# A decode attention on one core: 17 rounds of TensorE's loop, placed loops, and one load of keys that waits for the load ahead

## The chip, the cores and the metric

The kernel runs on one core of a Trainium2 chip. A core has five engines with instruction streams of their own: TensorE (PE; its weight loads, PEld, overlap its matmuls), VectorE (DVE), ScalarE (ACT), GpSimd (POOL) and SyncE (SP). Loads and stores go through 16 DMA engines that work side by side. Engines and transfers are tied together by semaphores alone. The metric is the device time of one execution in microseconds (us); lower is better.

## The reference

```python
B, Hq, Hkv, Sq, Sk, D = 1, 32, 8, 1, 65536, 128
k = jnp.repeat(k, rep, axis=1)          # rep = 4 query heads for each of 8 key heads
v = jnp.repeat(v, rep, axis=1)
scores = jnp.einsum("bhqd,bhkd->bhqk", q, k) * D ** -0.5
p = softmax(scores, axis=-1)
out = jnp.einsum("bhqk,bhkd->bhqd", p, v)
```

One query position for each of 32 heads attends to 65,536 keys and values of its key head. All is bf16. Keys and values are 134 MB each, and each is read once.

## The kernel before

The work is cut into NU = 32 units: 8 key heads, HU = 4 units for each. A unit is 16,384 keys: 128 partitions with T = 128 tiles each. Its keys are one load of 4 MB into one of two buffers (`kbuf`), its values another one of 4 MB into one of two (`vbuf`). Each partition's 32 KB are contiguous in memory.

SP issues the loads in the order k0, k1, v0, k2, v1, k3, v2 and so on (`sync_engine`, lines 378 to 411). A load into a buffer that was used waits for `kfree` or `vfree`: ScalarE raises `kfree` when the last of a unit's transposed keys is about to be copied, VectorE raises `vfree` when it takes a unit's result. A load's semaphore (`krdy`, `khalf`, `vrdy`) is complete at 16, one from each DMA engine. The first and the last load of keys come in two halves, the last load of values in six pieces (`V_PIECES`, in tiles) with semaphores `vpiece`.

TensorE runs a loop of 16 rounds (lines 200 to 207). A round has the keys of an even unit, the values of the odd unit before it (not in the first round), the keys of the odd unit, the values of the even one. `pe_keys` takes 16 groups of 8 tiles: it transposes a group's tiles against an identity into one of four PSUM banks (line 132), and three groups later multiplies the transposed keys with the head's four queries (line 141). `pe_values` multiplies 128 tiles of values with the weights into one small accumulator (line 158). Behind the loop, `pe_last` does the values of unit 31, piece by piece: it transposes the outputs of the other heads first (line 173), does a small sum between the first and second piece (line 178), and handles the last 8 tiles in another layout (line 191), so that the result of the last head needs no transpose.

VectorE and ScalarE copy the transposed keys out of PSUM (lines 219 and 216, ScalarE every fourth group). VectorE also takes the maximum of a unit's scores (line 248) and does the running softmax's bookkeeping; GpSimd reduces the maximum over partitions (line 369); ScalarE computes the exponentials (line 339). `passes` writes out the first passes of VectorE and ScalarE, then a loop whose body holds four passes (one head's units), then the rest. VectorE's loop runs the passes 1 to 28, seven iterations; pass u copies the keys of unit u + 1. GpSimd's and SP's streams have no loop: all 32 units are written out.

[...] The programs are fetched in blocks by DMA transfers that the profile lists as kind "instruction".

Of the kernel before, what the change touches and what calls it, by code (L numbers as in the profile page):

```python
# [10 lines left out]
P = 128  # L11
T = 128
# [5 lines left out]
HU = 4  # L18
HALF = T // 2

V_PIECES = (64, 32, 16, 8, 4, 4)
ROWS_FROM = 120


LOOP_SLOT = 176


def on_act(j):
# [3 lines left out]
def take(e, sem, n=1):  # L32

    e.wait_ge(sem, n)
    e.sem_inc(sem, -n)  # L35


def bass_standalone__gqa_softmax__decode_kernel(nc, q, k, v, out):
    _, Hq, _, D = q.shape
    _, H, Sk, _ = k.shape  # L40
    R = Hq // H
    HR = H * R
    NU = H * HU
    assert D == P and Sk == P * T * HU and T * R == 512 and H >= 3 and NU % 2 == 0
    scale = float(D) ** -0.5
    kf, vf, qf, of = k[0], v[0], q[0, :, 0, :], out[0, :, 0, :]
# [4 lines left out]
    def sb(name, shape, dt):  # L51
        return S(nc.sbuf_tensor(name, shape, dt))

    def sem(name):
        return S(nc.semaphore(name))

    kbuf = [sb(f"kbuf{i}", [P, T * D], DT.bfloat16) for i in range(2)]
    vbuf = [sb(f"vbuf{i}", [P, T * D], DT.bfloat16) for i in range(2)]
# [10 lines left out]
    ones = sb("ones", [P, 1], DT.float32)  # L69
# [8 lines left out]
    lp = sb("lp", [P, R], DT.float32)  # L78
# [12 lines left out]
    fin = pvb[NU % 2]  # L91
# [3 lines left out]
    vrdy = [sem(f"vrdy{i}") for i in range(2)]  # L95
    vpiece = [sem(f"vpiece{i}") for i in range(len(V_PIECES))]
# [3 lines left out]
    qkd, qrdy, pvd = sem("qkd"), sem("qrdy"), sem("pvd")  # L100
    cm, cma, ng, exd, sx, lrd, lra = (sem(n) for n in ("cm", "cma", "ng", "exd", "sx", "lrd", "lra"))
    xd, xa, xg = sem("xd"), sem("xa"), sem("xg")
    q_sem, o_sem, s_x, t_z, t_id, t_if, t_qT = (
        sem(n) for n in ("q_sem", "o_sem", "s_x", "t_z", "t_id", "t_if", "t_qT"))
    t_o, s_o, t_row, t_lp, s_l, t_acc, s_fin, t_last = (
        sem(n) for n in ("t_o", "s_o", "t_row", "t_lp", "s_l", "t_acc", "s_fin", "t_last"))


    def has_k(u):
        return u + 1 < NU  # L110

    def passes(e, one, start, period, last):

        for u in range(-1, start):
            one(u)
        n = (NU - 2 - start) // period
        with e.Fori(0, n):
            for u in range(start, start + period):
                one(u)
        for u in range(start + n * period, last + 1):  # L120
            one(u)
# [24 lines left out]
    def pe_keys(pe, b):  # L146
        pend = []
        for j in range(G):
            pe_transposes(pe, b, j)
            pend.append(j)  # L150
            if len(pend) > LAG:
                pe_scores(pe, b, pend.pop(0))
        while pend:
            pe_scores(pe, b, pend.pop(0))

    def value(pe, b, t, first, last):
        vv = vbuf[b][:, :].rearrange("p (t d) -> p t d", d=D)
        return pe.matmul(pvb[b][:, 0:R], lhsT=vv[:, t, :], rhs=pts[b][:, t * R:(t + 1) * R],  # L158
                         start=t == first, stop=t == last)

    def pe_values(pe, b):
        take(pe, vrdy[b], 16)
        take(pe, exd)
        for t in range(T):
            ins = value(pe, b, t, 0, T - 1)
        ins.then_inc(pvd, 1)

    def pe_last(pe):
        b = (NU - 1) % 2
        vv = vbuf[b][:, :].rearrange("p (t d) -> p t d", d=D)  # L170
        starts = [sum(V_PIECES[:i]) for i in range(len(V_PIECES))]
        pe.wait_ge(t_o, 1)
        pe.transpose(qkb[0][0:HR - R, 0:P], oT[:, R:HR], identf[:, :]).then_inc(s_o, 1)
        take(pe, exd)
        for t in range(ROWS_FROM):
            if t == starts[1]:
                pe.wait_ge(t_lp, 1)
                pe.matmul(fin[0:R, P:P + 1], lhsT=lp[:, :], rhs=ones[:, :],
                          start=True, stop=True).then_inc(s_l, 1)
            if t in starts:  # L180
                pe.wait_ge(vpiece[starts.index(t)], 16)
            ins = value(pe, b, t, 0, ROWS_FROM - 1)
        ins.then_inc(pvd, 1)
        pe.wait_ge(t_last, 1)
        for t in range(ROWS_FROM, T):
            if t in starts:
                pe.wait_ge(vpiece[starts.index(t)], 16)
            if t == starts[-1]:
                pe.wait_ge(t_acc, 1)
                pe.matmul(fin[0:R, 0:P], lhsT=acc[:, :], rhs=identf[:, :], start=False, stop=False)  # L190
            ins = pe.matmul(fin[0:R, 0:P], lhsT=pts[b][:, t * R:(t + 1) * R], rhs=vv[:, t, :],  # L191
                            start=t == ROWS_FROM, stop=t == T - 1)
        ins.then_inc(s_fin, 1)

    def tensor_engine(pe):
        pe.wait_ge(q_sem, 16)
        pe.wait_ge(t_id, 1)
        pe.transpose(trb[0][:, 0:HR], qsb[:, :], ident[0:HR, 0:HR]).then_inc(s_x, 1)  # L198
        pe.wait_ge(t_qT, 1)
        pe.addr_align(256, offset=LOOP_SLOT, max_nops=16)  # L200
        with pe.Fori(0, NU // 2) as i:
            pe_keys(pe, 0)
            with pe.If(i > 0):
                pe_values(pe, 1)
            pe_keys(pe, 1)
            pe_values(pe, 0)
        pe_last(pe)


# [11 lines left out]
    def own(e, ins, s):  # L221
        ins.then_inc(s, 1)
        take(e, s)
# [80 lines left out]
    def vector_engine(e):  # L304
        identities(e)
        e.memset(oT[:, :], 0.0).then_inc(xd, 1)
        take(e, xd)
        e.wait_ge(s_x, 1)
        own(e, e.tensor_copy(qT[:, :], trb[0][:, 0:HR]), xd)
        next_queries(e, t_qT)  # L310
        e.sem_inc(qrdy, 1)
        passes(e, lambda u: dve_pass(e, u), 1, HU, NU - 4)
        e.sem_inc(t_o, 1)
        for u in range(NU - 3, NU):
            dve_pass(e, u)
        e.sem_inc(t_lp, 1)
        e.wait_ge(s_o, 1)
        e.tensor_copy(orow[:, :], qkb[0][0:HR - R, 0:P]).then_inc(t_row, 1)
        e.wait_ge(s_l, 1)
        e.reciprocal(rl[:, :], fin[0:R, P:P + 1]).then_inc(t_last, 1)  # L320
        take(e, pvd)
        b = (NU - 1) % 2
        e.tensor_tensor(acc[:, :], acc[:, :], pvb[b][:, 0:R], ALU.add).then_inc(t_acc, 1)
        e.wait_ge(t_last, 1)
        e.wait_ge(s_fin, 1)  # L325
        e.tensor_scalar(olast[:, :], fin[0:R, 0:P], rl[:, 0:1], None, ALU.mult).then_inc(t_last, 1)  # L326
# [30 lines left out]
    def gpsimd_engine(e):  # L357
        e.memset(ident[:, :], 0.0)
        e.memset(identf[:, :], 0.0)
        e.memset(ones[:, :], 1.0)  # L360
        e.memset(dscr[:, :], 0.0)
        e.memset(la[:, :], 0.0).then_inc(t_z, 1)
        e.wait_ge(t_z, 1)
        e.partition_all_reduce(cmaxa[:, :], la[:, :], P, bass.bass_isa.ReduceOp.max).then_inc(xg, 1)
        for u in range(NU):
            if u == 0:
                e.wait_ge(xg, 1)
            take(e, cm)
            e.partition_all_reduce(cmaxa[:, :], cmax[:, :], P, bass.bass_isa.ReduceOp.max).then_inc(cma, 1)  # L369
            if u % HU == HU - 1 and has_k(u):  # L370
                take(e, lrd)
                e.partition_all_reduce(la[:, :], lp[:, :], P, bass.bass_isa.ReduceOp.add).then_inc(lra, 1)  # L372

    def src(x, n):
        h, c = n // HU, n % HU
        return x[h, c * P * T:(c + 1) * P * T, :].rearrange("(p t) d -> p (t d)", p=P)

    def sync_engine(e):
        def pieces(buf, s, sizes, sems):
            a = 0  # L380
            for w, sm in zip(sizes, sems):
                e.dma_start(buf[:, a * D:(a + w) * D], s[:, a * D:(a + w) * D]).then_inc(sm, 16)  # L382
                a += w

        def load_k(n):
            b = n % 2
            if n >= 2:
                e.wait_ge(kfree[b], n // 2)
            if n in (0, NU - 1):
                pieces(kbuf[b], src(kf, n), (HALF, T - HALF), (krdy[b], khalf[b]))  # L390
            else:
                e.dma_start(kbuf[b][:, :], src(kf, n)).then_inc(krdy[b], 16)
                e.sem_inc(khalf[b], 16)

        def load_v(n):
            b = n % 2
            if n >= 2:
                e.wait_ge(vfree[b], n // 2)
            if n == NU - 1:
                pieces(vbuf[b], src(vf, n), V_PIECES, vpiece)  # L400
            else:
                e.dma_start(vbuf[b][:, :], src(vf, n)).then_inc(vrdy[b], 16)

        load_k(0)
        for n in range(NU - 1):
            load_k(n + 1)
            load_v(n)
        load_v(NU - 1)
        e.wait_ge(t_last, 2)
        e.dma_start(of[HR - R:HR, :], olast[:, :]).then_inc(o_sem, 16)  # L410
        e.wait_ge(o_sem, 32)
# [35 lines left out]
```

## Time and profile before

| | |
|---|---|
| time, median of 3 runs | 633.15 us (633.11 to 633.5) |
| profiled execution's own time | 632.97 us |
| its span, first to last instruction | 631.2 us |
| TensorE matmuls / weight loads busy | 520.4 / 512.3 us |
| VectorE / ScalarE / GpSimd busy | 312.4 / 182.4 / 15.9 us |
| read from memory | 268.44 MB |
| mean granted TensorE clock | 0.772 |

In the profile, a row of the order of time has the start, the duration, the engine, the line and operation, the tiles written and read, the shape and count, and in brackets the idle time of the engine ahead of it with what ended it ("PEq" is TensorE's own instruction stream, which includes its waits on semaphores; "issue" is a wait for nothing that the profile shows). A row of a window has the window, its length, the busy time of each engine with a count, the granted clock, the share of the 16 DMA engines' time, and the rate in GB/s. A row of the transfer queues has packets, MB and the share of 16 engines' time: q1 is the loads' queue, the kind "instruction" is the programs'.

### The profile page before, as it was taken

The page shows a single profiled execution, that of the slowest core. Times are in us where ns is not written, and L with a number is a line of the kernel's source. Part 1 is how long each engine was busy: PE and PEld are TensorE (multiplying, and loading weights), DVE is VectorE, ACT ScalarE, POOL GpSimd, SP SyncE. Part 2 cuts the span into 40 slices and gives each one's busy share as a digit, 9 for nine tenths or more (in the row PEclk, how much of TensorE's full clock was granted, in tenths as well). Part 3 has the DMA queues.
Part 4 walks back from the last instruction along what each step waited for, and adds up shares of the span by engine and source line. Part 5 has one row for each costly group of instructions (what it writes and reads, how often), then busy time and mean ns, then how long its engine had stood idle before and what let it go on. Part 6 is the DMA issues. An engine that isn't in the chain of part 4 may idle for free. (4 is left out here: it accounts for less than half of the span.)

```text
span 631.2 us, 27735 instructions
## 1 busy us (share of the span) xinstructions
PE 520.4 (82%) x12294; PEld 512.3 (81%) x12294; DVE 312.4 (49%) x689; ACT 182.4 (29%) x410; POOL 15.9 (3%) x49
## 2 busy tenths in 40 slices
PE   4579998879887798878798787988779887879897
PEld 4479997879887788877798787988779877779896
DVE  4445554446544456434565344654445544455552
ACT  2133322123322233221332213332223322133231
POOL 0000000000000000000000000000000000000000
PEclk9788776778776788767887677877678876788776
DMA  8999999999999999999999999999999999999996
GB/s 366 429 432 431 430 430 432 432 432 432 432 432 432 432 432 432 432 432 432 432 432 432 432 432 432 432 432 432 432 432 430 432 432 432 432 432 432 424 437 255
DMA packets 10335, 268.62 MB, mean 426 GB/s; under 512 B 1234, under 2 KB 1490, under 8 KB 1746
## 3 DMA queue, kind: packets, MB, share of 16 engines
q1 hardware_dynamic: 10232, 268.44, 99.1%
q8 instruction: 7, 0.11, 0.1%
q14 instruction: 6, 0.05, 0.0%
q10 hardware_dynamic: 90, 0.02, 0.0%
HBM read 268.44 MB, written 0.01 MB: 425 GB/s over the span
## 5 line engine op out<-in xcount | busy, mean ns | idle before, releaser
L132 PE MATMUL trb<-ident,kbuf 128*128 128x128 bf16 x4096 | 357.1, 246 | 76.1 <-PEq L35 73.3
L132 PEld LDWEIGHTS trb<-ident,kbuf 128*128 128x128 bf16 x4096 | 289.8, 112 | 78.0 <-issue 77.8
L219 DVE COPY ktb<-trb 128x1024 bf16<-128x1024 bf16 x384 | 255.2, 691 | 164.2 <-DVEq L35 163.5
L216 ACT ACTIVATE ktb<-trb 128x1024 bf16<-128x1024 bf16 x128 | 131.0, 1023 | 436.0 <-ACTq L35 436.0
L141 PE MATMUL qkb<-qcur,ktb 128*128 128x4 bf16 x4096 | 173.3, 165 | 22.5 <-PEq L35 20.5
L141 PEld LDWEIGHTS qkb<-qcur,ktb 128*128 128x128 bf16 x4096 | 156.3, 98 | 26.2 <-issue 26.0
L158 PE MATMUL pvb<-pts,vbuf 128*128 128x4 bf16 x4088 | 112.1, 165 | 4.9 <-issue 1.7
L158 PEld LDWEIGHTS pvb<-pts,vbuf 128*128 128x128 bf16 x4088 | 110.0, 101 | 6.8 <-issue 4.3
L339 ACT ACTIVATE pts<-qkb,negm 128x128 bf16<-128x128 f32 x128 | 50.8, 551 | 0.0
L248 DVE TENSOR_REDUCE cmax<-qkb 128x4 f32<-128x512 f32 x32 | 22.1, 692 | 35.2 <-DVEq L35 34.2
L339 ACT ACTIVATION_READ_ACCUMULATOR pts<-qkb,negm 128x1 f32 x128 | 36.1, 282 | 0.0
L237 DVE TENSOR_TENSOR acc<-acc,pvb 128x4 f32<-128x4 f32 x23 | 3.7, 159 | 59.8 <-DVEq L35 59.8
L369 POOL PARTITION_ALL_REDUCE cmaxa<-cmax x32 | 11.9, 370 | 506.3 <-POOLq L35 506.3
L235 DVE COPY acc<-pvb 128x4 f32<-128x4 f32 x8 | 1.3, 162 | 23.8 <-DVEq L35 23.8
L226 DVE COPY qcur<-qT 128x4 bf16<-128x4 bf16 x8 | 1.4, 170 | 10.0 <-DVEq L35 9.9
L278 DVE TENSOR_TENSOR lp<-lp,rsum 128x4 f32<-128x4 f32 x24 | 3.9, 163 | 3.5
L277 DVE TENSOR_TENSOR lp<-lp,alpha 128x4 f32<-128x4 f32 x24 | 3.9, 163 | 3.5
L264 DVE TENSOR_TENSOR dm<-m 128x4 f32<-128x4 f32 x24 | 3.9, 163 | 3.5
L335 ACT ACTIVATE alpha<-dm 128x4 f32<-128x4 f32 x24 | 4.7, 197 | 2.7 <-ACTq L35 2.7
L372 POOL PARTITION_ALL_REDUCE la<-lp x7 | 3.0, 429 | 97.0 <-POOLq L35 97.0
L198 PE MATMUL trb<-ident,qsb 32*128 32x32 bf16 x1 | 0.2, 204 | 5.1 <-DMA qsb<-in_q_dram 5.1
L198 PEld LDWEIGHTS trb<-ident,qsb 32*128 32x128 bf16 x1 | 0.1, 100 | 5.1 <-DMA qsb<-in_q_dram 5.1
(43 smaller groups left out, 32.7 us busy)
## 6 DMA issues: line engine op xcount, KB each, us to landing
vbuf<-in_v_dram SPq DMA_DIRECT2D x31, 4096.0 KB, 31.4
kbuf<-in_k_dram SPq DMA_DIRECT2D x30, 4096.0 KB, 26.8
kbuf<-in_k_dram SPq DMA_DIRECT2D x4, 2048.0 KB, 17.1
vbuf<-in_v_dram SPq DMA_DIRECT2D x1, 2048.0 KB, 17.7
vbuf<-in_v_dram SPq DMA_DIRECT2D x1, 1024.0 KB, 19.8
vbuf<-in_v_dram SPq DMA_DIRECT2D x1, 512.0 KB, 20.3
vbuf<-in_v_dram SPq DMA_DIRECT2D x1, 256.0 KB, 20.5
vbuf<-in_v_dram SPq DMA_DIRECT2D x2, 128.0 KB, 20.2
```

Of the source, the lines that this page charges most:

```text
L132: ins = pe.transpose(trb[j % NTB][:, i * P:(i + 1) * P], kv[:, t, :], ident[:, :])
L141: ins = pe.matmul(qkb[b][:, t * R:(t + 1) * R], lhsT=ktb[:, off:off + P], rhs=qcur[:, :], start=True, stop=True)
L158: return pe.matmul(pvb[b][:, 0:R], lhsT=vv[:, t, :], rhs=pts[b][:, t * R:(t + 1) * R], start=t == first, stop=t == last)
L216: e.activation(dst, trb[j % NTB][:, :], AF.Copy).then_inc(eva, 1)
L219: e.tensor_copy(dst, trb[j % NTB][:, :]).then_inc(evd, 1)
L248: e.tensor_reduce(cmax[:, :], qkb[u % 2][:, :].rearrange("p (t g) -> p g t", g=R), AX.X, ALU.max).then_inc(cm, 1)
L264: e.tensor_tensor(dm[:, :], mo[:, :], mn[:, :], ALU.subtract)
L277: own(e, e.tensor_tensor(lp[:, :], lp[:, :], alpha[:, :], ALU.mult), xd)
L278: own(e, e.tensor_tensor(lp[:, :], lp[:, :], rsum[:, :], ALU.add), xd)
L335: e.activation(alpha[:, :], dm[:, :], AF.Exp, scale=scale)
L339: ins = e.activation(pv[:, g, :], sv[:, g, :], AF.Exp, bias=negm[:, g:g + 1], scale=scale, accum_out=rsum[:, g:g + 1])
L369: e.partition_all_reduce(cmaxa[:, :], cmax[:, :], P, bass.bass_isa.ReduceOp.max).then_inc(cma, 1)
```

## The change

TensorE's loop starts at the beginning of a block of 256 and runs 17 rounds. Its round is now four conditional parts: keys of the even unit (not in round 17), values of the odd unit before it (not in the first round; in round 17 the first 64 tiles alone), then keys of the odd unit and values of the even one (neither in round 17). So the first 64 tiles of the last unit's values are multiplied by the loop's code, and `pe_last` starts with the transpose of the outputs and the small sum, and goes on at tile 64. The first piece of the last values signals `vrdy` like a whole load.

VectorE's loop is placed at 208 of 256; GpSimd's passes, and SP's loads from the second round of its order on, start at the beginning of a block of 128.

SP splits value load 4 into pieces of 102 and 26 tiles with semaphores of their own. Key load 6 is issued only when the first piece has landed on all 16 DMA engines. SP then waits for the second piece as well, raises `vrdy` for the whole load itself, and issues value load 5.

```diff
+BLOCK_PE = 256
+BLOCK = 128
+MEET = 4
+MEET_TILES = 26
+DVE_SLOT = 208
...
+    meet = [sem(f"meet{i}") for i in range(2)]
...
-    def passes(e, one, start, period, last):
+    def passes(e, one, start, period, last, align=None):
...
         n = (NU - 2 - start) // period
+        if align:
+            align()
         with e.Fori(0, n):
...
-    def pe_values(pe, b):
-        take(pe, vrdy[b], 16)
-        take(pe, exd)
-        for t in range(T):
+    def pe_values(pe, b, t0, t1):
+        if t0 == 0:
+            take(pe, vrdy[b], 16)
+            take(pe, exd)
+        for t in range(t0, t1):
             ins = value(pe, b, t, 0, T - 1)
-        ins.then_inc(pvd, 1)
+        if t1 == T:
+            ins.then_inc(pvd, 1)
...
         pe.transpose(qkb[0][0:HR - R, 0:P], oT[:, R:HR], identf[:, :]).then_inc(s_o, 1)
-        take(pe, exd)
-        for t in range(ROWS_FROM):
-            if t == starts[1]:
-                pe.wait_ge(t_lp, 1)
-                pe.matmul(fin[0:R, P:P + 1], lhsT=lp[:, :], rhs=ones[:, :],
-                          start=True, stop=True).then_inc(s_l, 1)
+        pe.wait_ge(t_lp, 1)
+        pe.matmul(fin[0:R, P:P + 1], lhsT=lp[:, :], rhs=ones[:, :],
+                  start=True, stop=True).then_inc(s_l, 1)
+        for t in range(HALF, ROWS_FROM):
...
-        pe.addr_align(256, offset=LOOP_SLOT, max_nops=16)
-        with pe.Fori(0, NU // 2) as i:
-            pe_keys(pe, 0)
+        pe.addr_align(BLOCK_PE, max_nops=0)
+        n = NU // 2
+        with pe.Fori(0, n + 1) as i:
+            with pe.If(i < n):
+                pe_keys(pe, 0)
             with pe.If(i > 0):
-                pe_values(pe, 1)
-            pe_keys(pe, 1)
-            pe_values(pe, 0)
+                pe_values(pe, 1, 0, HALF)
+                with pe.If(i < n):
+                    pe_values(pe, 1, HALF, T)
+            with pe.If(i < n):
+                pe_keys(pe, 1)
+                pe_values(pe, 0, 0, T)
         pe_last(pe)
...
-        passes(e, lambda u: dve_pass(e, u), 1, HU, NU - 4)
+        passes(e, lambda u: dve_pass(e, u), 1, HU, NU - 4,
+               lambda: e.addr_align(2 * BLOCK, offset=DVE_SLOT, max_nops=0))
...
+        e.addr_align(BLOCK, max_nops=0)          # GpSimd, ahead of its passes
         for u in range(NU):
...
+            if n == MEET + 2:                    # in load_k
+                e.wait_ge(meet[0], 16)
...
-                pieces(vbuf[b], src(vf, n), V_PIECES, vpiece)
+                pieces(vbuf[b], src(vf, n), V_PIECES, [vrdy[b]] + vpiece[1:])
+            elif n == MEET:
+                pieces(vbuf[b], src(vf, n), (T - MEET_TILES, MEET_TILES), meet)
...
             load_k(n + 1)
+            if n == MEET + 1:
+                e.wait_ge(meet[1], 16)
+                e.sem_inc(vrdy[MEET % 2], 16)
             load_v(n)
+            if n == 0:
+                e.addr_align(BLOCK, max_nops=0)
```

More of the change, by code (lines that the diff above doesn't have):

```diff
@@ L22 @@
 ROWS_FROM = 120
-LOOP_SLOT = 176
+BLOCK_PE = 256
[3 more added lines that the diff above has]
+DVE_SLOT = 208
 def on_act(j):
```

## The prediction

> **What bounds the kernel now.** I read the page first (span, transfer rate, the chain that ended last), then the order of time on TensorE where it starts on a load of keys, then the transfer rate in short windows at the end, then the transfer queues in windows.
>
> ```profile
> span 631.2 us, 27735 instructions
> ...
> PE 520.4 (82%) x12294; PEld 512.3 (81%) x12294; DVE 312.4 (49%) x689; ACT 182.4 (29%) x410; POOL 15.9 (3%) x49
> ...
> GB/s 366 429 432 431 430 430 432 432 432 432 432 432 432 432 432 432 432 432 432 432 432 432 432 432 432 432 432 432 432 432 430 432 432 432 432 432 432 424 437 255
> ...
> q1 hardware_dynamic: 10232, 268.44, 99.1%
> ...
> q8 instruction: 7, 0.11, 0.1%
> q14 instruction: 6, 0.05, 0.0%
> ...
> DMA vbuf<-in_v_dram 3%; SPq L382 0%; PE pvb L191 0%; PE pvb L190 0%; PE pvb L158 0%; DVE olast L326 0%; DVEq L232 0%; DVEq L325 0%
> ```
>
> No compute engine is full, the rate stands at 432 GB/s in nearly every slice, the queue of loads (q1) fills 99.1% of the 16 DMA engines, and the chain ends in the load of the last values. 268.44 MB at 432 GB/s is 621.4 us of the 631.2. The kernel is a stream of loads. A load counts as landed when all 16 engines have added to its semaphore, so the engine that is last sets the end. The other two queues, 13 packets called "instruction", bring the engines' programs, over the same 16 engines.
>
> TensorE's rows, from four stretches of the order of time, show how late the last engine gets:
>
> ```profile
> 8.26 1.01 PE L132 MATMUL trb<-ident,kbuf 128*128 128x128 bf16 x8 [2.94 <-PEq L35]
> ...
> 102.14 3.57 PE L132 MATMUL trb<-ident,kbuf 128*128 128x128 bf16 x32 [2.22 <-PEq L35]
> ...
> 587.86 1.44 PE L132 MATMUL trb<-ident,kbuf 128*128 128x128 bf16 x12 [2.88 <-PEq L35]
> ...
> 627.24 0.29 PEld L158 LDWEIGHTS pvb<-pts,vbuf 128*128 128x128 bf16 x8 [0.16 <-DMA vbuf<-in_v_dram]
> ```
>
> These are starts that waited for a landing: the first half of key load 0, key load 5, key load 30, and the fourth piece of the last values. From load 5 to load 30 lie 50 loads: (587.86 - 102.14) / 50 = 9.714 us each. By that pace, load 5 (9.5 loads after the first half) should come at 8.26 + 92.3 = 100.5; it comes 1.6 us later. The fourth piece ends 8 tiles of 128 short of four loads after load 30: 587.86 + 38.86 - 0.61 = 626.1; it comes 1.1 us later. So the last engine lost about 2.7 us, 1.6 early and 1.1 at the end.
>
> The rate in short windows at the end (last number of each line; the one before it is the share of the engines' time) shows that it was indeed one engine:
>
> ```profile
> 624.00:624.50 0.50, 0.50 (x25) 0.50 (x23) 0.00 (x0) 0.00 (x0) 0.00 (x0) 0.50 0.99 367
> ...
> 625.50:626.00 0.50, 0.50 (x24) 0.50 (x23) 0.00 (x0) 0.00 (x0) 0.00 (x0) 0.50 0.48 166
> ...
> 626.50:627.00 0.50, 0.42 (x16) 0.42 (x16) 0.00 (x0) 0.00 (x0) 0.00 (x0) 0.50 0.06 23
> ...
> 627.00:627.50 0.50, 0.42 (x15) 0.34 (x11) 0.00 (x0) 0.00 (x0) 0.00 (x0) 0.50 0.06 19
> ```
>
> One engine's share of 432 is 27 GB/s. The first engines are done soon after 624, under half are left at 625.75, and for the last us before 627.5 a single one works (share 0.06, one in 16).
>
> What delayed it? The queues in the windows 13 to 60, 110 to 600 and 604 to 607 us (packets, MB, share of 16 engines' time):
>
> ```profile
> q8 instruction: 6, 0.10, 0.8%
> ...
> q14 instruction: 2, 0.02, 0.0%
> ...
> q14 instruction: 1, 0.01, 0.7%
> ```
>
> Nine of the program's packets lie there: six of 16 KB early (0.8% of 47 x 16 us, 1.0 us each on its engine), two in the long middle, and one of 8 KB at 605 (0.7% of 48 us, 0.34 us). That last one is the only one in the stretch in which the last engine lost 1.1 us, so I price an 8 KB fetch, with what it upsets, at 1.1. The other two in the middle fell on engines that were ahead: the 50 loads keep their pace.
>
> **The change, part by part.** *Loops placed, early branches, 17 rounds.* This takes away TensorE's and VectorE's waits for code, such as these:
>
> ```profile
> 25.79 3.04 PE L132 MATMUL trb<-ident,kbuf 128*128 128x128 bf16 x27 [3.20 <-PEq L35]
> ...
> 31.64 0.44 PE L132 MATMUL trb<-ident,kbuf 128*128 128x128 bf16 x5 [2.81 <-issue]
> ...
> 46.32 3.09 PE L158 MATMUL pvb<-pts,vbuf 128*128 128x4 bf16 x111 [1.69 <-issue]
> ...
> PE trb L132 <- PEq L35: 73.3, 28, 3.3
> ```
>
> They are worth nothing on the path: TensorE goes on to wait for keys 28 times, 2.6 us each (last row), and the stream does not stop for it. The three added branches a round lie in the same waits. If that cover were gone, a round would lose at most one such 2.8.
>
> *The end of the program.* The first 64 tiles of the last values become round 17; the transpose of the outputs and the small sum, earlier before and between the pieces, come behind them.
>
> ```profile
> 621.65 0.37 PE L173 MATMUL qkb<-identf,oT 128*28 128x128 f32 x1
> ...
> 622.84 1.87 PE L158 MATMUL pvb<-pts,vbuf 128*128 128x4 bf16 x64 [0.82 <-DMA vbuf<-in_v_dram]
> ...
> 624.64 0.19 PE L178 MATMUL pvb<-ones,lp 128*4 128x1 f32 x2
> ...
> 625.35 1.01 PE L158 MATMUL pvb<-pts,vbuf 128*128 128x4 bf16 x32 [0.52 <-DMA vbuf<-in_v_dram]
> ```
>
> The piece ends near 624.6; 0.37 and 0.19 us follow, in a gap of 0.5. A branch or two can make the next piece 0.2 to 0.5 late, and the 0.16 to 0.3 us that TensorE waits before each of the two pieces behind it take that back: 0. A late entry here would cost 2.8 less about 1.1 of such gaps, +1.7, and I take 0 because the code left behind the loop is shorter by 64 tiles. The transposed outputs go out about 1 us later, hidden by the final store.
>
> *Fetches moved.* VectorE's loop body, counted from the code, is some 180 instructions for four passes. The diff aligns by 128 instructions, on TensorE by 256, and the packets are of 8 and 16 KB: I take a packet as one such block. Put at slot 208 of 256, it ends just inside the block (from slot 384) that then also holds the tail, so the 605 fetch goes to the end of the loop's first iteration, whose last copies are these:
>
> ```profile
> 112.55 1.99 DVE L219 COPY ktb<-trb 128x1024 bf16<-128x1024 bf16 x3 [0.53 <-DVEq L35]
> ...
> 605.18 0.16 DVE L237 TENSOR_TENSOR acc<-acc,pvb 128x4 f32<-128x4 f32 x1 [2.51 <-DVEq L35]
> ```
>
> GpSimd's and SP's fetches go to the first microseconds. A moved fetch still takes its 0.34 us, and its 1.1, from the engine that carries it; if that engine is the last one, it is as late as before. Price: 0, with -1.1 as the other end (it falls on another engine, or while its engine idles) and +1.1 (on an engine that is last already).
>
> *The hold.* Key load 6 waits for 102 of the 128 tiles of value load 4; value load 5 then waits for the rest.
>
> ```profile
> 94.78 0.33 SPq L392 DMA_DIRECT2D kbuf<-in_k_dram  x1
> ...
> 100.10 0.33 SPq L402 DMA_DIRECT2D vbuf<-in_v_dram  x1
> ...
> 114.49 0.33 SPq L392 DMA_DIRECT2D kbuf<-in_k_dram  x1
> ...
> DMA to landing us min/median/max: 7.4/26.7/27.9
> ...
> qsb<-in_q_dram ACTq DMA_DIRECT2D x1, 8.0 KB, 4.3
> ```
>
> Key load 6 was issued at 94.78; value load 4 lands one load after 102.1, at 111.9, and its first 102 tiles 26/128 x 9.71 = 1.97 us before, so the issue moves to 109.9. Behind it on SP's queue stand value load 5 (100.10 to 111.9, not wanted before key load 6 has streamed until 121.6) and key load 7 (114.49, not moved). TensorE's values 4 get their signal from SP, after 111.9, and are due after keys 5, near 116. What the hold costs the last engine is what an issue needs to reach data, less 1.97. The fastest 2 MB piece took 7.4, 2.5 more than its 4.85 at 432 GB/s: 0.6 of stall. The 8 KB load took 4.3: 2.3 of stall. Not at all is the other end. The 2 MB piece is the nearer kind, and part of its 2.5 lies behind its last byte: I take +0.3. The engines ahead lose up to 2 us, which is free.
>
> What does the hold give? All engines go on in step. No view shows what that is worth; long windows bound it:
>
> ```profile
> 110.00:200.00 90.00, 74.10 (x1808) 73.09 (x1807) 43.52 (x93) 24.95 (x54) 2.28 (x6) 0.77 1.00 431
> ...
> 420.00:470.00 50.00, 41.55 (x1056) 40.91 (x1052) 24.50 (x53) 14.41 (x29) 1.11 (x3) 0.79 1.01 433
> ```
>
> If nothing, 0. If engines in step all ran at 433 instead of 431 over the 516 us behind the hold: -2.4. I take -0.9, nearer to nothing, because VectorE's last fetch comes at about 113 or later, behind the hold, and its engine falls out of step again.
>
> [...]
>
> **The sum.** 0 + 0 + 0 + 0.3 - 0.9 = -0.6 against the profiled execution's 632.97 (its 631.2 of span and 1.8 around it), which stands 0.18 under the median of 633.15. On the median: 632.5.
>
> **The rivals.** *In step and clean:* the last fetch lies ahead of the hold or does no harm, and the late 1.1 us is not lost again. Then -0.9 to -2.4 from the step, and the 0.3: about -1.8, 631.3. For it: every other fetch can lie before 110. Against: the 112.55 row, which dates the loop's end behind the hold. *Delays add:* before the change, a delay on one engine hides behind a larger one on another. The hold makes all wait for the slowest, and the next fetch comes on top. It decides if the slowest at the hold is another engine than the one VectorE's fetch falls on: 1.1 more, and the 0.3, +1.4: 634.6. For it: the loss of 1.6 before the hold. Against: if one engine carries all of VectorE's fetches, nothing is added. *Loop refetched:* VectorE's loop now reaches into three blocks; if the first is gone when it branches back, each of six back edges costs a fetch of 1.1, 639.7. Against: TensorE's loop of some 1,580 slots branches back 15 times, and the window from 110 to 600 holds no 16 KB packet. [...] *The change doesn't do it:* the late fetch stays, the step is worth nothing: 633.1.
>
> **How the numbers follow.** Forecast (a small gain, 632.0 to 633.0) 0.40; no effect 0.08; in step and clean 0.33; delays add 0.14; refetched 0.05. The range 631.0 to 634.0 holds the first three, 0.81. About 0.2% (1.27 us) is what a measurement of this kernel can tell from no change: faster 0.33, within it 0.48, slower 0.19.
>
> **What would show it.** Right: no program packet after about 120; key load 6 issued near 110, its landing not late; the end with one engine alone for a us or more still; keys 5 to 30 at 9.70 us a load or a little less. In step and clean: a pace of 9.68, and all engines finishing within 1 us. Delays add: the same pace, and the single engine's stretch at the end as long as the whole loss. Refetched: a program packet in every iteration of eight loads (78 us). It would be wrong by most if TensorE's exit from the loop waited for code.

## The result, and the profile after

The changed kernel takes 634.98 us (median of 11 executions, 634.49 to 635.73), the kernel before 633.07 in the same comparison: a ratio of 1.003, 95% interval 1.0023 to 1.0038. It is 1.9 us slower, 0.3%. The profiled execution takes 634.92 us, 2.4 more than its span of 632.5. Before, the span was 631.2 and the rest 1.8.

The page of the changed kernel, in the lines that answer those shown of before:

```profile
span 632.5 us, 27796 instructions
...
GB/s 367 433 429 432 430 428 406 420 435 433 431 431 433 431 433 431 431 431 431 431 431 433 431 431 431 431 431 431 431 433 431 433 433 431 433 431 431 426 432 264
...
q1 hardware_dynamic: 10376, 268.44, 98.9%
q8 instruction: 7, 0.11, 0.1%
q14 instruction: 6, 0.05, 0.0%
...
DMA vbuf<-in_v_dram 3%; SPq L398 0%; PE pvb L200 0%; PE pvb L199 0%; PE pvb L167 0%; DVE olast L341 0%; DVEq L246 0%; DVEq L340 0%
```

The kernel is still a stream of loads whose last landing sets the end. A dip stands in the seventh and eighth slice (406 and 420 GB/s, from 95 to 126 us), where the hold lies.

The order of time of the changed kernel: three starts of TensorE that waited for a landing (key loads 5, 6 and 30), and the last result on VectorE.

```profile
102.29 1.44 PE L141 MATMUL trb<-ident,kbuf 128*128 128x128 bf16 x12 [0.79 <-PEq L41]
...
123.80 2.51 PE L141 MATMUL trb<-ident,kbuf 128*128 128x128 bf16 x22 [4.95 <-PEq L41]
...
590.18 2.08 PE L141 MATMUL trb<-ident,kbuf 128*128 128x128 bf16 x18 [3.15 <-PEq L41]
...
630.59 0.34 DVE L341 TENSOR_SCALAR olast<-pvb,rl 4x128 bf16<-4x128 f32 x1 [1.29 <-PE pvb L200]
```

The same view of the kernel before, in the two rows that the prediction didn't need:

```profile
121.56 3.57 PE L132 MATMUL trb<-ident,kbuf 128*128 128x128 bf16 x32 [2.13 <-PEq L35]
...
629.22 0.34 DVE L326 TENSOR_SCALAR olast<-pvb,rl 4x128 bf16<-4x128 f32 x1 [1.30 <-PE pvb L191]
```

With load 5 at 102.14 and load 30 at 587.86 (quoted in the prediction) these rows cut both executions into the same pieces, and the pieces account for the whole difference of the two profiled executions, 634.92 - 632.97 = 1.95 us:

| piece | before | after | difference |
|---|---|---|---|
| start to key load 5 | 102.14 | 102.29 | +0.15 |
| key load 5 to 6, two loads | 19.42 | 21.51 | **+2.09** |
| key load 6 to 30, 48 loads | 466.30 | 466.38 | +0.08 |
| key load 30 to the last result | 41.36 | 40.41 | **-0.95** |
| last result to the end of the span | 1.98 | 1.91 | -0.07 |
| outside the span | 1.77 | 2.42 | **+0.65** |

The late loss of the kernel before (0.95 behind load 30) is gone. Two loads at the hold cost 2.09 more, and the end outside the span 0.65 more. The pace between is what it was: 466.38 / 48 = 9.716 us a load, against 9.715.

What lies at the hold? SP's issues in the order of time, and the rate in one window of both kernels (first the kernel before, then the changed one; the last number is GB/s):

```profile
109.99 0.33 SPq L410 DMA_DIRECT2D kbuf<-in_k_dram  x1
111.99 0.33 SPq L422 DMA_DIRECT2D vbuf<-in_v_dram  x1
```

```profile
100.00:124.00 24.00, 19.05 (x408) 18.92 (x409) 10.62 (x21) 5.58 (x12) 0.37 (x1) 0.71 1.00 429
```

```profile
100.00:124.00 24.00, 17.62 (x444) 17.36 (x441) 9.33 (x19) 5.58 (x12) 0.37 (x1) 0.71 0.97 402
```

Key load 6 is issued at 109.99, and value load 4 has landed at 111.99 at the latest, when SP goes on to value load 5. The engines' mean loses (429 - 402) / 432 x 24 = 1.5 us.

The transfer queues of the changed kernel in three windows: 115 to 118 us, 120 to 632, and from 632.5 on, behind the span's last instruction.

```profile
q14 instruction: 1, 0.01, 0.6%
...
q1 hardware_dynamic: 8393, 218.67, 99.3%
q10 hardware_dynamic: 42, 0.01, 0.0%
...
q14 instruction: 1, 0.01, 0.3%
```

VectorE's 8 KB fetch, at 605 before, comes between 115 and 118. From 120 to 632 there is no program packet at all. One more 8 KB packet comes after the last instruction; the kernel before has no packet in that window.

### The profile page after: what moved, and what is told of

It reads as the page before. It is cut to its first block, busy times and chain, and to the rows that moved or that the text cites. A ratio compares the mean times of both kernels' runs of the same rounds, so it can differ in the third digit from the quotient of the medians.

```text
span 632.5 us, 27796 instructions
## 1 busy us (share of the span) xinstructions
PE 519.8 (82%) x12294; PEld 511.9 (81%) x12294; DVE 311.6 (49%) x689; ACT 182.7 (29%) x410; POOL 15.9 (3%) x49
```

## The experiments

Four questions: what does the hold cost, does it give anything, what does VectorE's fetch cost where it now lies, and where do the 0.65 us outside the span come from? The table has every run beside its measurement. Medians and ratios are of 11 executions each (7 of kernel 3) against the kernel before on the same chip (633.02 to 633.11). The pieces are those of the table above, one profiled execution each, and stretches in which nothing was changed agree to about 0.1 us; "outside" is the median of time less span.

| kernel | median us | ratio, interval | load 5 to 6 | 6 to 30 | 30 to last result | outside |
|---|---|---|---|---|---|---|
| before | 633.11 | 1 | 19.42 | 466.30 | 41.36 | 1.83 |
| changed | 634.98 | 1.003 [1.0023, 1.0038] | 21.51 | 466.38 | 40.41 | 2.39 |
| 1 hold alone, 26 tiles | 633.83 | 1.0012 [1.0003, 1.0021] | 20.24 | 466.48 | 41.13 | 1.83 |
| 2 hold alone, 64 tiles | 633.07 | 1.0001 [0.9992, 1.001] | 19.50 | 466.23 | 40.92 | 1.82 |
| 3 hold alone, 4 tiles | 635.06 | 1.0033 [1.0022, 1.0044] | 21.57 | 466.89 | 40.45 | 1.80 |
| 4 changed, no hold | 633.52 | 1.0006 [0.9997, 1.0015] | 20.41 | 466.33 | 40.77 | 2.37 |
| 5 changed, hold of 64 tiles | 633.67 | 1.0009 [1.0, 1.0018] | - | 466.24 | 40.37 | 2.36 |
| 6 changed, hold at load 8 | 634.25 | 1.0021 [1.0012, 1.003] | 20.40 | 466.86 | 40.48 | 2.37 |
| 7 before, short VectorE program | 632.14 | 0.9984 [0.9975, 0.9993] | 19.43 | 466.31 | 40.40 | 1.78 |
| 8 changed, short VectorE program | 633.26 | 1.0003 [0.9994, 1.0012] | 20.49 | 466.26 | 40.43 | 1.81 |
| 9 no hold, VectorE not placed | 632.99 | 1.0 [0.9991, 1.0009] | 19.42 | 466.30 | 41.22 | 1.79 |
| 10 no hold, short VectorE program | 632.05 | 0.9986 [0.9977, 0.9995] | 19.42 | 466.29 | 40.41 | 1.80 |

(In kernel 5 TensorE did not wait for load 5, so that the piece can't be read.)

A second table is worked out from the trace's records of the semaphores that the loads' 16 engines raise: by how many us the last engine is behind the 15th, and behind the first. (These records, and those of single packets that are used below, are in the trace but in none of the views.)

```
kernel                        value load 4      key load 6       last piece of values
                              15th   first      15th   first     15th   first
before                        0.04   1.92       0.05   1.93      1.01   2.84
changed                       0.31   2.09       1.36   2.09      1.50   2.11
1 hold alone, 26 tiles        0.24   2.07       0.05   0.92      0.70   1.73
3 hold alone, 4 tiles         0.23   2.13       0.03   0.53      0.02   1.08
4 changed, no hold            0.39   2.27       1.37   3.25      1.46   3.22
6 changed, hold at load 8     0.20   2.01       1.17   2.99      0.01   0.52
7 short VectorE program       0.16   2.07       0.17   2.07      0.19   2.01
8 changed, short VectorE      0.23   2.02       0.20   0.95      0.18   0.90
10 no hold, short VectorE     0.14   1.97       0.12   1.96      0.19   1.91
```

### What the hold costs: kernels 1, 2 and 3

Kernel 1 adds the hold, and nothing else, to the kernel before. Kernels 2 and 3 do the same with `MEET_TILES` 64 and 4: the issue then comes 4.86 and 0.30 us before value load 4 has landed, instead of 1.97 (tiles / 128 x 9.71).

```diff
+MEET = 4
+MEET_TILES = 26          # kernel 2: 64, kernel 3: 4
...
+            if n == MEET + 2:
+                e.wait_ge(meet[0], 16)
...
+            elif n == MEET:
+                pieces(vbuf[b], src(vf, n), (T - MEET_TILES, MEET_TILES), meet)
...
+            if n == MEET + 1:
+                e.wait_ge(meet[1], 16)
+                e.sem_inc(vrdy[MEET % 2], 16)
```

> The kernel before with the hold alone: value load 4 in pieces of 102 and 26 tiles, key load 6 held for the first of them. No placing of loops, 16 rounds. Theory A (the hold itself stops the last engine, because a load that is issued late needs longer than the 1.97 us of cover to reach full pace): span 1.0 to 1.4 us longer than the 631.2 of before, the time about 634.3, keys 5 to keys 6 about 1.2 us further apart than 9.71 a load, and the time outside the span stays 1.8. Theory B (the hold costs nothing, a fetch behind it is what adds): 633.1 to 633.4, since here VectorE's last fetch comes at 605 as before and its engine is last in both. Theory C (engines in step run faster): below 632.5.

> The kernel before with the hold alone, but 64 tiles (4.9 us) still to come when key load 6 is let go, in place of 26 (2.0 us). If the hold costs because engines run dry and start again slowly: no engine runs dry, cost 0, time 633.0 to 633.2, and the engines stay as far apart as before. If it costs because value load 4 comes in two pieces or because SP has two more waits: 633.8 as with 26 tiles.

> The kernel before with the hold alone and 4 tiles (0.3 us) still to come. If engines running dry is the price: 1.7 us less cover, so about 1.7 more than the 633.8 with 26 tiles, 635.2 to 635.7. If the price is a fixed one for a restart: 633.8 to 634.2.

TensorE's starts on key loads 5 and 6, in the order of time of kernels 1, 2 and 3; of kernel 3 also SP's issue of key load 6:

```profile
102.30 1.44 PE L136 MATMUL trb<-ident,kbuf 128*128 128x128 bf16 x12 [3.01 <-PEq L38]
...
122.54 3.57 PE L136 MATMUL trb<-ident,kbuf 128*128 128x128 bf16 x32 [3.39 <-PEq L38]
```

```profile
102.46 1.33 PE L136 MATMUL trb<-ident,kbuf 128*128 128x128 bf16 x11 [1.30 <-PEq L38]
...
121.96 3.57 PE L136 MATMUL trb<-ident,kbuf 128*128 128x128 bf16 x32 [3.04 <-PEq L38]
```

```profile
102.22 1.54 PE L136 MATMUL trb<-ident,kbuf 128*128 128x128 bf16 x13 [2.31 <-PEq L38]
...
123.79 2.50 PE L136 MATMUL trb<-ident,kbuf 128*128 128x128 bf16 x22 [5.36 <-PEq L38]
...
111.57 0.33 SPq L398 DMA_DIRECT2D kbuf<-in_k_dram  x1
```

Against 19.42 for the two loads, the hold costs 0.08 with a cover of 4.86 us (the time by which the issue comes ahead of value load 4's landing), 0.82 with 1.97, and 2.15 with 0.30. Cover and stall together are 1.97 + 0.82 = 2.8 and 0.30 + 2.15 = 2.45 us. A cover of 2 us is too short, and one of 4.9 is enough.

That time is not all a way from issue to data. By the trace's packet records the 16 engines begin their first packet of key load 6 at 0.96 to 1.93 us after the issue in kernel 1, and at 0.95 to 1.54 us in kernel 3. This first packet of 32 KB takes 1.27 to 2.01 us in kernel 1 and 1.52 to 2.20 us in kernel 3, the next one on each engine 1.21 to 1.22. In the changed kernel they begin 0.96 to 2.08 us after the issue, and the first packet takes 1.30 to 2.36 us, the next one 1.21 to 1.22 on 14 of the 16 engines. So a part of the stall is a slow first packet; why it is slow stays open. The splitting of the load, the two waits on SP and the signal that SP raises cost nothing, since kernel 2 has them all and takes 633.07. In the median the hold alone costs 0.7 us, between what theory A (1.2) and theory B (0 to 0.3) had expected.

The second table shows what the hold does to the order of the engines: with 26 tiles the last one is then 0.92 behind the first instead of 2.07, and with 4 tiles 0.53. They are nearly in step. Kernel 3 even reads its last piece with 0.02 between the last two engines: VectorE's fetch at the end, which costs 0.95 before, lies on an engine that the restart had left ahead (load 30 to last result 40.45). It is of no use to it: 2.15 lost, 0.91 regained at the end, and 0.6 more lost between loads 6 and 30. Two program packets of 8 KB lie in that stretch, as before, and they are where the 0.6 goes: in kernel 3 they come at 413.0 and 457.0, and just behind each of them the last engine lands a load 10.03 us after the load ahead, where all other loads of the stretch take 9.70 to 9.73. In the kernel before, the same two packets (411.8 and 472.7) cost nothing: no landing is late there, so their engines were ahead of the last one.

### Hold and fetch taken apart: kernels 4, 8 and 10

Kernel 4 is the changed kernel without the hold.

```diff
-            if n == MEET + 2:
-                e.wait_ge(meet[0], 16)
...
-            elif n == MEET:
-                pieces(vbuf[b], src(vf, n), (T - MEET_TILES, MEET_TILES), meet)
...
-            if n == MEET + 1:
-                e.wait_ge(meet[1], 16)
-                e.sem_inc(vrdy[MEET % 2], 16)
```

Kernel 8 keeps the hold, but VectorE's loop is not placed, and it runs the passes 29 and 30 in an eighth, half skipped iteration. Its program is some 90 instructions shorter (counted from the code), and of the passes the last alone stands behind the loop. Kernel 10 has this VectorE program and no hold. Kernel 7 is the kernel before with this VectorE program alone; it shows whether the late fetch is what costs the last 0.95 us.

```diff
-        passes(e, lambda u: dve_pass(e, u), 1, HU, NU - 4, ...)
-        e.sem_inc(t_o, 1)
-        for u in range(NU - 3, NU):
-            dve_pass(e, u)
+        for u in range(-1, 1):
+            dve_pass(e, u)
+        n = (NU - 3) // HU
+        with e.Fori(0, n + 1) as i:
+            for u in (1, 2):
+                dve_pass(e, u)
+            with e.If(i < n):
+                for u in (3, 4):
+                    dve_pass(e, u)
+        e.sem_inc(t_o, 1)
+        dve_pass(e, NU - 1)
```

> The kernel before with VectorE's passes 29 and 30 done by an eighth iteration of its loop (half of it skipped there), which makes its program some 90 instructions shorter, so that it does not reach the block whose entry brought the fetch at 605. Theory A (the last engine is the one that carries VectorE's fetches, each about 1 us): no program packet near 605, the end 1.0 us earlier, about 632.1, and the single engine's stretch at the end gone. If the late fetch is not what makes that engine last: 633.1.

> The changed kernel without the hold: placed loops, 17 rounds, value load 4 in one piece. Theory A: the moved fetch takes from the last engine what it took at 605, so the span is 631.2 plus or minus 0.2; what lies outside the span is 2.4 as in the changed kernel, so the time is 633.6 to 633.9. Theory B: the same. If the placing were what lengthens the span, the span would be near 632.5 and the time near 634.9.

> The changed kernel with VectorE's shorter program (passes 29 and 30 in an eighth iteration, loop not placed), so that no third fetch of VectorE comes behind the hold. Theory A (terms simply add): the span of the changed kernel less 1.0, about 631.6. Theory B (a fetch just behind the hold costs 0.7 beyond its own 1.0): less 1.7, about 630.9. The time outside the span tells whether VectorE's place brought the 0.6 there: 1.8 if so, 2.4 if it is TensorE's, SP's or GpSimd's.

> The changed kernel without the hold, and with VectorE's passes 29 and 30 run by its loop and its program not placed: the program is some 90 instructions shorter and should end in the block that the loop's end lies in. Against the changed kernel without the hold (633.52, span 631.1, 2.37 outside it) two things should go. If VectorE's third fetch costs the last engine its whole time wherever no stall hides it, 1.0 goes from the span (630.1); and if the 0.6 outside the span comes from VectorE's place, the outside is 1.8 again. Then 631.9. If the fetch is only paid because the engines are where the placed streams put them, the span stays at 631.1 and the time is 632.9. If the placed programs of the other engines cost by themselves, it stays over the 632.14 of the kernel before with the short VectorE program by as much.

(These are, in order, the kernels 7, 4, 8 and 10.) Kernel 7 first, its load 30 and its last result in the order of time, and two windows of the end:

```profile
587.93 3.57 PE L132 MATMUL trb<-ident,kbuf 128*128 128x128 bf16 x32 [2.05 <-PEq L35]
...
628.33 0.34 DVE L333 TENSOR_SCALAR olast<-pvb,rl 4x128 bf16<-4x128 f32 x1 [1.30 <-PE pvb L191]
```

```profile
626.00:626.50 0.50, 0.44 (x16) 0.36 (x14) 0.00 (x0) 0.00 (x0) 0.00 (x0) 0.50 0.22 69
626.50:627.00 0.50, 0.45 (x11) 0.39 (x10) 0.13 (x1) 0.00 (x0) 0.00 (x0) 0.50 0.01 1
```

The stretch from 626.5 to 627.5, in which a single engine worked before (share 0.06), is gone, the piece is 40.40 instead of 41.36, and the kernel takes 632.14, 1.0 less. So the fetch at 605 does cost about 1.0, as priced.

The packet records show what makes 1.0 of it. In the kernel before, the 8 KB program packet takes 0.32 us from 605.53 on, and the 16 KB data packet that begins as it ends takes 1.27 us, where the others of its size take 0.61. That is 0.32 + 0.66 = 0.98 of one engine. What the stream loses is that, less what this engine was ahead of the last one. In kernels 1, 2 and 9, where the same fetch comes near 605 too, the last engine was 0.25, 0.43 and 0.13 us behind the 15th just before it, and the landing behind it is 0.72, 0.51 and 0.85 late: together 0.94 to 0.98 each time.

Now the two loads at the hold, in the order of time of kernels 4, 8 and 10:

```profile
102.30 1.44 PE L141 MATMUL trb<-ident,kbuf 128*128 128x128 bf16 x12 [0.45 <-PEq L41]
...
122.71 3.57 PE L141 MATMUL trb<-ident,kbuf 128*128 128x128 bf16 x32 [3.73 <-PEq L41]
```

```profile
102.20 1.55 PE L141 MATMUL trb<-ident,kbuf 128*128 128x128 bf16 x13 [1.85 <-PEq L41]
...
122.69 3.20 PE L141 MATMUL trb<-ident,kbuf 128*128 128x128 bf16 x32 [4.32 <-PEq L41]
```

```profile
102.00 1.76 PE L141 MATMUL trb<-ident,kbuf 128*128 128x128 bf16 x15 [2.44 <-PEq L41]
...
121.42 3.30 PE L141 MATMUL trb<-ident,kbuf 128*128 128x128 bf16 x32 [2.31 <-PEq L41]
...
587.71 3.57 PE L141 MATMUL trb<-ident,kbuf 128*128 128x128 bf16 x32 [3.05 <-PEq L41]
...
628.12 0.34 DVE L347 TENSOR_SCALAR olast<-pvb,rl 4x128 bf16<-4x128 f32 x1 [1.31 <-PE pvb L200]
```

| two loads, us | without the hold | with the hold |
|---|---|---|
| without VectorE's fetch near 116 | 19.42 (kernel 10) | 20.49 (kernel 8) |
| with it | 20.41 (kernel 4) | 21.51 (changed) |

The fetch costs 0.99 and 1.02, the hold 1.07 and 1.10: they add, to the 2.09 of the changed kernel. (Kernel 8's span of 631.3 lies between its theories, 631.6 and 630.9; the pieces decide for A, that the terms simply add.) The medians say the same with a wider uncertainty (each has some 0.6 us of it): the hold costs 633.26 - 632.05 = 1.2 without VectorE's placed program and 634.98 - 633.52 = 1.5 with it. In kernel 4 the last engine goes from 0.39 to 1.37 behind the 15th with the fetch, and stays there to the end. Its profiled execution is 0.65 above its median, with 0.4 of that behind load 30. There TensorE was late, and not the loads: the last result came 1.74 us behind the last landing, where it comes 1.37 behind it in the changed kernel and in kernel 9. TensorE began the values of unit 30 at 619.96 (618.23 in kernel 9), and its granted clock from 608 to 612 was 0.56 (1.00 in kernel 9).

### Does the hold give anything: kernels 5 and 6

Kernel 5 is the changed kernel with `MEET_TILES = 64`. Kernel 6 has `MEET = 6`: the hold then comes at key load 8, behind VectorE's fetch, with no program packet after it.

> The changed kernel with 64 tiles still to come when key load 6 is let go. If all of the 1.5 us between it (634.98) and the same without a hold (633.52) comes from engines running dry: 633.4 to 633.7. If a part comes from the split load or SP's waits just ahead of VectorE's third fetch: 633.9 to 634.9.

> The changed kernel with the hold two units later (value load 6, key load 8), behind VectorE's last fetch at 116. Theory A: the last engine has all three fetches ahead of the hold and then loses the same 1.2 us there: span 632.5, time 634.9, no gain although all engines then go on in step; at the end no stretch with one engine alone. Theory B (the fetch behind the hold adds): the addition goes, 633.6 to 633.9. Theory C (in step and clean is faster): 631.5 to 633.

Kernel 5 takes 633.67, within the noise of no hold at all (633.52): with a cover of 4.86 us the hold neither costs nor gives. Kernel 6 is the cleaner test, since nothing upsets the engines after its hold. Its key loads 7, 8 and 30 in the order of time, and its end in windows:

```profile
141.96 3.57 PE L141 MATMUL trb<-ident,kbuf 128*128 128x128 bf16 x32 [2.91 <-PEq L41]
...
161.90 3.57 PE L141 MATMUL trb<-ident,kbuf 128*128 128x128 bf16 x32 [3.13 <-PEq L41]
...
589.39 2.82 PE L141 MATMUL trb<-ident,kbuf 128*128 128x128 bf16 x25 [3.17 <-PEq L41]
```

```profile
627.00:627.50 0.50, 0.43 (x16) 0.35 (x14) 0.00 (x0) 0.00 (x0) 0.00 (x0) 0.50 1.05 353
627.50:628.00 0.50, 0.40 (x15) 0.32 (x13) 0.00 (x0) 0.00 (x0) 0.00 (x0) 0.50 0.50 156
628.00:628.50 0.50, 0.45 (x11) 0.39 (x11) 0.09 (x1) 0.00 (x0) 0.00 (x0) 0.50 0.02 3
```

All engines are busy until 627.5 (share 1.05), and little is left after 628 (share 0.02): in step to the last us, 0.52 between the first and the last. And the pace is (589.39 - 161.90) / 44 = 9.716 us a load, that of the kernel before. The rate in a long window is the same as well, here first for the kernel before, then for kernel 6:

```profile
160.00:580.00 420.00, 350.42 (x8302) 346.00 (x8303) 211.78 (x459) 123.24 (x279) 10.35 (x27) 0.77 1.00 432
...
160.00:580.00 420.00, 349.90 (x8269) 345.38 (x8270) 209.76 (x458) 123.25 (x279) 10.36 (x27) 0.76 1.00 432
```

So engines in step are not faster. The kernel is 0.7 slower than without the hold, and 0.5 of that is the restart at load 8 (161.90 - 141.96 = 19.94 for the two loads, instead of 19.42). With 634.25 it lies between theory A (634.9) and theory B (633.6 to 633.9), since this stall was 0.5 and not 1.2.

### The end outside the span: kernel 9

Kernel 9 is kernel 4 with VectorE's loop not placed.

```diff
-        passes(e, lambda u: dve_pass(e, u), 1, HU, NU - 4,
-               lambda: e.addr_align(2 * BLOCK, offset=DVE_SLOT, max_nops=0))
+        passes(e, lambda u: dve_pass(e, u), 1, HU, NU - 4)
```

> The changed kernel without the hold and without the placing of VectorE's loop; TensorE's 17 rounds and the places of the other streams stay. If VectorE's place alone brings the 0.6 outside the span, that is 1.8 again and the time is 632.9 to 633.1, the kernel before's: the fetch comes back to about 605 and costs there what it costs at 116. If the 0.6 comes from TensorE's or SP's or GpSimd's program instead, it stays 2.4 and the time 633.5.

The outside goes from 2.37 back to 1.79, the program packet behind the span is gone, and the fetch is at the end again, where it costs 0.81 (41.22 less 40.41). The queue of programs from 600 to 609 us, load 30 and the last result:

```profile
q14 instruction: 1, 0.01, 0.2%
...
588.02 3.22 PE L141 MATMUL trb<-ident,kbuf 128*128 128x128 bf16 x32 [2.39 <-PEq L41]
...
629.24 0.34 DVE L340 TENSOR_SCALAR olast<-pvb,rl 4x128 bf16<-4x128 f32 x1 [1.30 <-PE pvb L200]
```

The time is 632.99, the kernel before's. So the 0.6 outside the span belongs to VectorE's place alone, and TensorE's 17 rounds, the branches and the places of GpSimd and SP are worth nothing measurable. Over all kernels the median outside is 2.36 to 2.39 where VectorE is placed, and 1.78 to 1.83 where it isn't. A few single executions without the placing have 2.2 to 2.5 as well (three of 29 of the kernel before, on one chip), so that the place is not the only thing that can bring it. The packet behind the span takes 0.50 us from 634.66 on in the changed kernel; what it brings, and whether the end of the execution waits for it, is not shown.

Kernels 7 and 10 beat both the kernel before and the changed one: 632.14 and 632.05 us, 0.16% and 0.14% below the kernel before, each with an interval that excludes 1. Between the two lies all that the change does beside the hold and VectorE's place, and it is worth nothing that these runs can tell.

## Why the prediction was wrong

The forecast was 632.5, from 0 + 0 + 0 + 0.3 - 0.9; 634.98 was measured. Between the two profiled executions the forecast was -0.6, and +1.95 came. Of the 2.55 us between these, 0.9 is a gain from engines in step that did not come, 0.8 is a hold that cost 1.1 and not 0.3, 0.65 is time outside the span for which the sum had no term, and 0.2 is the start and the moved fetch. Step by step:

- *What bounds the kernel*: right. The stream sets the end, and one engine that is late sets the stream's. Kernel 7 shows it: without the fetch at 605 the end comes 1.0 us earlier. The reading that this fetch is the only one behind load 30 overlooked a 16 KB packet at 624.56; kernel 7 keeps that one, at 624.54, and loses nothing by it.
- *Late entries of TensorE, 0*: right. Kernel 9 has the 17 rounds and the branches and takes the time of before. TensorE's exit from its loop cost nothing: key load 30 to the last result is 40.41 in the changed kernel and 40.40 in kernel 7, with the old loop and no late fetch either.
- *Fetches moved, 0*: right in the sum, and by the way described. The fetch went from 605 to 116, behind the hold, and costs 1.0 there instead of 0.95. The 8 KB block was priced at 1.1, from the loss as a whole; the packet records give 0.98. That the two prices cancel hangs on which engine carries the fetch: in kernel 2, where the last engine was 0.43 behind the 15th, it costs 0.51. And the step looked at the start of VectorE's program and at its loop, and not at what lies behind the span: **the 0.6 us outside the span were in no term and in no rival.** The profile of before couldn't show them, and I set what lies around the span at 1.8 for both kernels without saying why it should stay.
- *The hold, +0.3*: mis-sized. It measured 0.8 (kernel 1) to 1.1 (kernel 8), inside the 0 to 2.3 given. The form was right (a need, less the cover of 1.97): my 0.3 made 2.3 us of the need, and it was 2.45 (kernel 3) to 3.07 (the changed kernel). But the need is not only what an issue takes to reach data. In kernel 1 all 16 engines had begun key load 6 by 1.93 us after the issue, which by that reading would have cost nothing; the slow first packet (1.27 to 2.01 us in kernel 1, the next one 1.21 to 1.22) was in no term. The reason that I gave for going below 0.6, that part of the 2 MB piece's time lies behind its last byte, pushed the value the wrong way: value load 4's landing, up to which the cover is counted, also lies behind its last data packet, by 0.45 us in kernel 1 (111.46 to 111.91).
- *Engines in step, -0.9*: wrong. It is 0 (kernel 6, in step from load 8 on, at 9.716 us a load). The bound for it was one window of 431 against one of 433 GB/s; over 160 to 580 us the rate is 432 in the kernel before and in kernel 6. A window of 50 or 90 us was too short a ruler for half a per cent.
- *Loop refetched*: refuted. From 120 to 632 there is no program packet, though VectorE's loop, some 180 instructions, and TensorE's, some 1,580 (both counted from the code), branch back.
- *Delays add*, 634.6: nearest to the time, and right that a stall and a fetch come on top of each other. Its mechanism is not: it made the sum depend on the hold, which takes away the lead behind which the fetch would hide. Without any hold the fetch costs 0.99 as well (kernel 4). The hold brings only its own 1.1.

With the measured terms the sum is 0.15 for the start, 1.1 for the hold, 1.0 - 0.95 for the moved fetch and 0.65 outside the span, which makes the 1.95 between the two profiled executions.

The signs that I named came as follows: no program packet from 120 to the end of the span, key load 6 issued at 109.99, and one engine alone at the end (1.50 us behind the 15th) were right; its landing was 2.09 late and the pace 9.716, and these two were to decide between a gain and a loss.

## What to carry to other kernels

In a stream that fills all transfer engines, ask of each stall and each program fetch on which engine it falls, and how far that engine is ahead of the last one: only what goes beyond this lead was paid here (of 0.94 to 0.98 us, 0.72, 0.51 and 0.85 where the lead was 0.25, 0.43 and 0.13). On the last engine that was all of it, and moving the fetch along the stream changed nothing; the shorter program took it away. A wait that lets the engines run dry was paid too, unless the next transfer was issued well ahead (4.9 us were enough, with 0.08 lost, and 2.0 were not, with 0.82), and lining the engines up earned nothing: the rate was 432 GB/s either way. When a program is placed, read the time outside the span too: with VectorE's placed it was 2.36 to 2.39 us, without 1.78 to 1.83.

## What the runs showed of the hardware

- VectorE's 8 KB program packet at 605 takes 0.32 us of its engine in the kernel before, and the data packet that begins as it ends takes 1.27 us instead of 0.61. The stream is put back by 0.95 to 1.0 where this falls on the last engine, and by less where the engine is ahead: load 30 to the last result is 0.72, 0.51, 0.81 and 0.04 longer in kernels 1, 2, 9 and 3 than the 40.41 of kernel 10.
- Behind the hold the 16 engines begin the next load 0.95 to 2.08 us after its issue (kernels 1 and 3 and the changed kernel), and their first packet of 32 KB takes 1.27 to 2.36 us, where 1.21 to 1.22 follow on nearly all engines. The hold brings them closer together: in kernel 1 they were 2.07 us apart before the hold and 0.92 behind it, in kernel 3 0.53. Why the first packet is slow stays open.
- VectorE's place changed the time outside the span by 0.6 us (2.37 in kernel 4, 1.79 in kernel 9), and with it one 8 KB program packet comes behind the last instruction, at 634.66 in the changed kernel.
- The 1.6 us that the last engine lost before key load 5 are there in every kernel in which the start can be read (load 5 starts between 102.00 and 102.46). No kernel took away the early 16 KB program packets (six from 13 to 60 us in the kernel before), so where the 1.6 comes from is not shown.
